# Linear attention and a gated feed-forward block: from the third batch on, k's work runs a pair ahead of q's, z is summed by block turns and spread by DMA, and kv is turned along with q'

## The chip, the cores and the metric

The kernel runs on one core of a Trainium2 chip. The core has five engines that run side by side: TensorE (PE, matrix products, with its weight loads PEld), VectorE (DVE), ScalarE (ACT), GpSimd (POOL) and SyncE (SP), whose only work here is to issue transfers (DMA). Each engine takes its own instructions strictly in order and waits on semaphores for the others. The metric is the device time of one execution in microseconds, as a median of several runs.

## The reference, cut to what matters

```python
# q, k, v: [8 batches, 8 heads, 576 tokens, 64]; omega: [128, 64]
def phi(x):
    h = x @ omega.T - sum(x * x) / 2          # [576, 128]
    return exp(h - max(h)) / sqrt(128)
q_p, k_p = phi(q * scale), phi(k * scale)
kv  = k_p.T @ v                               # [128, 64] of each head
z   = sum(k_p, over the tokens)               # [128]
out = (q_p @ kv) / (q_p @ z + 1e-06)          # [576, 64]
x   = out with heads side by side             # [4608, 512]
y   = ((x @ w_a) * (x @ w_b)) @ w_out         # w_a, w_b: [512, 1536]
```

Everything is float32. The feed-forward products split each operand into two parts (a high and a low one) and add three products.

## The kernel before, in words

Heads are worked on two at a time: a *pair* u = 4 x batch + hp, 32 pairs in all. A pair's 1152 tokens lie as nine chunks of 128, the ninth (the two tails of 64 tokens) shared by the batch in the tiles htk and htq. The feed-forward block of a batch (MoE) needs the x of its four pairs; the attention of the next batch runs beside it, put between the MoE's matmuls.

The order is not written out by hand. The code makes a graph of operations with costs, priorities and buffer slots; `Graph.schedule` (L132) plays it through with its own estimates and writes each engine's instructions in the order that comes out. A margin on an operation (MARGIN, BACK, SUMS) says how much later than its inputs the planner lets it start. SP issues all loads and stores in one queue, in that order.

The steps of a pair in `pair` (L494), for pairs 4 to 31:

- Loads: X holds k and q of the pair with the 64 dimensions on partitions, k on partitions 0 to 63 and q on 64 to 127; natk, natq hold them by token; v.
- `four` (L442): projection, four chunks of k and of q at a time, as products ppk and ppq that run side by side in the two halves of the array; maxima, sums of squares and exp give the tiles hk and hq.
- z: POOL adds hk's chunks (z, zs, six adds), giving 128 partial sums for each feature. ACT and DVE split these into a high and a low part (zr), PE multiplies both by a matrix of ones (pz, L572 and L573), so that the sum over the tokens stands on all partitions, and ACT copies that to zb.
- kv (L588): ten small products into pkv. ACT copies it to k2, PE transposes that (pk, L598), ACT copies it to kl.
- Division: DVE takes the dot product of each chunk of hq with zb (L609, ten for a pair), inverts (L614, L615), and ACT scales hq by it (L619). The result is called q' here.
- The turn of q': DVE turns blocks of 32 x 32 (L627, tile qd), four DMAs write qd to DRAM (qdr, L637), one DMA loads it back into hq, and together that is a transpose. Pair 7 does it on PE instead.
- num: pm (L647) and a short tail (L649) multiply kl with q'. They are not issued alone but right behind the kv products of the next pair (`pending`), so that PE changes to these matmuls once for both. The result goes to the MoE's x.

The MoE of batches 2 to 8 (`moe_block7`) makes products of six matmuls (L1047) in two banks of PSUM, which DVE adds up into c (L1057), and then the output products o (L785). Batch 8 stands for the tails of all.

Of the kernel before, what the change touches and what calls it, by code (L numbers as in the profile page):

```python
# [7 lines left out]
F32 = mybir.dt.float32  # L8
# [9 lines left out]
P = 128  # L18
# [37 lines left out]
class Graph:  # L56
# [3 lines left out]
    def __init__(self):  # L60
        self.ops, self.rings, self.slots = [], {}, {}
# [50 lines left out]
    def place(self, o):  # L112

        t, got = 0, []
        for b in o.alloc:
# [4 lines left out]
            for s in [*ring["slots"], *b.more]:  # L120
# [113 lines left out]
def tile_attention_moe(ctx: ExitStack, tc: tile.TileContext, kqt, kqtt, kqn, kqnt, vx, omst, idn, wab, wout, out):  # L234
# [20 lines left out]
    LATE = dict(wo=["h0", "h1"], ot=["X0", "X1", "h2", "qd0"], owr=["raw0", "raw1"], og=["nat0", "nat1", "ht0", "ht1"], ogf=["xf0", "xf1"],  # L255
# [35 lines left out]
    junk = fixed([P, M], mybir.dt.bfloat16, "junk")  # L291
# [5 lines left out]
    zero = fixed([P, P], mybir.dt.bfloat16, "zero")  # L297
# [69 lines left out]
    qdram = [dram.tile([4, 32, 4, NCH * 32], F32, name=f"qdr{i}") for i in range(3)]  # L367
    qdram_b = [g.buf(None, None, None, f"qdr{i}") for i in range(3)]
    xtd = dram.tile([NHP, P, B * TL], F32, name="xtd")
# [72 lines left out]
    def four(nm, b, pri, x, xdep, dst, c0, sm, sq, al, deps, mg, more):  # L442
# [51 lines left out]
    def pair(u, gate):  # L494
# [59 lines left out]
        def zadd(eng, n, o, a, c, r, w, al=()):  # L554
            g.op({"POOL": pool2(n)}, lambda e: ENG[e].tensor_tensor(o(), a(), c(), op=ALU.add), r=r, w=w, alloc=list(al), prio=pri)  # L555
# [10 lines left out]
        hi, lo = (lambda: zr.ap[:, 0]), (lambda: zr.ap[:, 1])
        g.op({"ACT": act(2 * M)}, copier(hi, lambda: flat(zs)), r=[(zs, None)], w=[(zr, 0)], alloc=[zr], prio=pri + 9)
        g.op({"DVE": dve(2 * M)}, subber(lo, lambda: flat(zs), hi), r=[(zs, None), (zr, 0)], w=[(zr, 1)], prio=pri + 9)
        pz = g.buf("at", [P, 2 * M], F32, f"pz{nm}", more)

        def broadcast(e):
            nc.tensor.matmul(pz.ap[:], ones.ap[:], hi(), start=True, stop=False)  # L572
            nc.tensor.matmul(pz.ap[:], ones.ap[:], lo(), start=False, stop=True)  # L573
        g.op({"PE": mm(2, 2 * M)}, broadcast,
             r=[(zr, None), (ones, None)], w=[(pz, None)], alloc=[pz, zb], prio=pri + 10, margin=mg and mg + CFG["SUMS"])
# [654 lines left out]
```

## Time and profile before

| | us |
|---|---|
| median of three runs | 1074.24 |
| lowest and highest | 1074.06, 1075.35 |
| the profiled execution: its time | 1071.77 |
| the profiled execution: its span | 1070.0 |
| granted TensorE clock, share of full | 1.00 |
| DMA, mean rate | 286 GB/s |

The profile is of one execution. Its page gives the busy time of each engine, forty slices of the span with the busy share in tenths, the chain of work that ended last, and groups of instructions by line, operation and tile with count, busy time, mean length in nanoseconds, and the idle time before them with what ended it. Names of tiles are shown without their numbers: p stands for both MoE banks, c for all sums. Other views answer for one stretch of time (windows, timeline), for one engine's waits, or for one tile.

### The profile page before, as it was taken

To read this page: it belongs to the slowest core of one execution; us is meant where nothing else is said; L and a number is where in the kernel's file an instruction comes from. 1 tells how busy PE (TensorE), PEld (TensorE's weight loads), DVE (VectorE), ACT (ScalarE), POOL (GpSimd) and SP (SyncE) were. 2 spreads that over 40 slices of the span, in tenths; PEclk is the share of its full clock that TensorE was granted. 3 is DMA by queue.
4 is the path that set the end of the run, shared out by engine and by line. 5 is a ranking of instruction groups with operands and counts; after the bars stand their busy time and mean duration, and the time that the engine had idled before them with its cause. 6 is when DMAs were issued, how large, how long until landed. Compare 5 with 4: busy or idle time off the path is not lost.

```text
span 1070.0 us, 22015 instructions
## 1 busy us (share of the span) xinstructions
PE 1053.8 (98%) x7899; PEld 928.8 (87%) x7899; DVE 867.2 (81%) x2145; ACT 591.1 (55%) x1599; POOL 106.4 (10%) x176
## 2 busy tenths in 40 slices
PE   9999999999999999999999999999999999999997
PEld 7878777868788889888888988888888989999997
DVE  6999986989886788777886879778876777998766
ACT  7997767666764646554645566464645423333111
POOL 0021111111110101010111111010101000000000
PEclk9999999999999999999999999999999999999999
DMA  9877966797898888978888888988796799999991
GB/s 359 306 240 230 335 198 208 243 377 274 283 320 295 276 301 269 339 264 289 295 312 295 273 298 270 332 265 299 257 323 196 261 334 304 319 336 344 352 305 50
DMA packets 118270, 305.61 MB, mean 286 GB/s; under 512 B 16656, under 2 KB 35856, under 8 KB 118160
## 3 DMA queue, kind: packets, MB, share of 16 engines
q1 hardware_dynamic: 117296, 303.55, 82.8%
q8 instruction: 62, 1.02, 0.4%
q10 hardware_dynamic: 864, 0.66, 0.2%
q14 instruction: 48, 0.39, 0.1%
HBM read 249.43 MB, written 54.72 MB: 284 GB/s over the span
## 4 chain that ended last, share of the span: by engine, by line
PE 82%; DVE 7%; ACT 5%; DMA 3%; issue 1%; POOL 1%; SPq 0%; ACTq 0%; DVEq 0%
PE p L1047 34%; PE o L785 19%; PE ppk L452 5%; PE pb L956 5%; PE pa L956 5%; PE o_P L853 4%; PE pkv L588 3%; PE pm L647 2%; DMA td<-ts 1%; DVE c L1057 1%; ACT hq L619 1%; ACT hk L486 1%; DMA out_dram<-osb 1%; PE p L853 1%; PE pn L720 1%
## 5 line engine op out<-in xcount | busy, mean ns | idle before, releaser
L1057 DVE TENSOR_TENSOR c<-p,c 128x512 f32<-128x512 f32 (+1 forms) x336 | 207.7, 618 | 93.0 <-PE p L1047 86.7
L785 PE MATMUL o<-wo,ghl 128*128 128x512 f32 x1008 | 270.6, 397 | 0.3 <-DVE ghl L282 0.3
L785 PEld LDWEIGHTS o<-wo,ghl 128*128 128x128 f32 x1008 | 175.5, 188 | 32.0 <-DVE ghl L282 1.2
L1047 PE MATMUL p<-Sa,t 128*128 128x256 f32 x1008 | 144.6, 281 | 1.6 <-ACT c L274 1.6
L1047 PEld LDWEIGHTS p<-Sa,t 128*128 128x128 f32 x1008 | 133.1, 188 | 7.6 <-ACT c L274 2.4
L555 POOL TENSOR_TENSOR z<-hk 128x256 f32<-128x256 f32 x56 | 45.2, 807 | 690.3 <-ACT hk L486 488.9
L274 ACT COPY c<-p 128x256 f32<-128x256 f32 x84 | 31.1, 371 | 125.9 <-PE p L1047 72.7
L486 ACT ACTIVATE hk<-hk,sm 128x128 f32<-128x128 f32 x192 | 62.3, 392 | 46.7 <-DVE sm L482 38.7
L619 ACT ACTIVATE hq<-hq,dn 128x128 f32<-128x128 f32 x224 | 70.6, 392 | 26.6 <-DVE dn L615 24.9
L956 PE MATMUL pb<-x,wb 128*128 128x512 f32 x288 | 75.2, 401 | 0.0
L956 PE MATMUL pa<-x,wa 128*128 128x512 f32 x288 | 73.7, 398 | 0.9 <-DVE x L282 0.9
L1047 PE MATMUL p<-Sb,t 128*128 128x256 f32 x504 | 74.5, 283 | 0.0
L1047 PE MATMUL p<-Sb,bq 128*128 128x256 f32 x504 | 74.5, 283 | 0.0
L1047 PE MATMUL p<-x,t 128*128 128x256 f32 x504 | 73.7, 282 | 0.7 <-ACT oc L274 0.7
L1047 PEld LDWEIGHTS p<-x,t 128*128 128x128 f32 x504 | 69.1, 188 | 5.9 <-ACT oc L274 1.1
L452 PE MATMUL ppk<-om,X 64*128 64x128 f32 x512 | 73.9, 285 | 0.0
L452 PE MATMUL ppq<-om,X 64*128 64x128 f32 x512 | 73.4, 284 | 0.1
L452 PEld LDWEIGHTS ppk<-om,X 64*128 64x128 f32 x512 | 61.7, 187 | 13.5 <-issue 3.4
L1047 PE MATMUL p<-x,wb 128*128 128x256 f32 x504 | 71.2, 284 | 1.6 <-DVE c L1057 1.5
L609 DVE CUSTOM_DVE_ANT_0 junk<-hq,zb 128x128 bf16<-128x128 f32 x224 | 65.6, 293 | 8.6 <-ACT zb L274 6.5
L1047 PE MATMUL p<-x,wa 128*128 128x256 f32 x504 | 71.2, 286 | 1.0 <-DVE c L1057 0.9
L1047 PEld LDWEIGHTS p<-x,wb 128*128 128x128 f32 x504 | 65.9, 188 | 5.1 <-DVE c L1057 2.0
(185 smaller groups left out, 2027.5 us busy)
## 6 DMA issues: line engine op xcount, KB each, us to landing
t<-td SPq DMA_DIRECT2D x168, 512.0 KB, 5.6
wo<-wod SPq DMA_DIRECT2D x96, 512.0 KB, 5.8
bq<-bd SPq DMA_DIRECT2D x84, 256.0 KB, 5.6
X<-in_kqt_dram SPq DMA_DIRECT2D x31, 512.0 KB, 5.7
qdr<-qd SPq DMA_DIRECT2D x108, 144.0 KB, 4.3
hq<-qdr SPq DMA_DIRECT2D x27, 576.0 KB, 6.5
raw<-in_wab_dram SPq DMA_DIRECT2D x24, 512.0 KB, 6.2
td<-ts SPq DMA_DIRECT2D x24, 512.0 KB, 5.9
```

The source lines that it names most:

```text
L274: nc.scalar.copy(o(), i())
L452: nc.tensor.matmul(pps[w].ap[:, c * M:c * M + M], x()[rows, c * P:c * P + P], om.ap[rows], start=True, stop=True)
L486: g.op({"ACT": 392}, lambda e, c=c, w=w: nc.scalar.activation(dst[w].ap[:, c], src[w](c), AF.Exp, scale=SC, bias=sm.ap[:, 2, w, c:c + 1]), ...
L555: g.op({"POOL": pool2(n)}, lambda e: ENG[e].tensor_tensor(o(), a(), c(), op=ALU.add), r=r, w=w, alloc=list(al), prio=pri)
L588: nc.tensor.matmul(pkv.ap[D * j:D * j + D, 0:M], vb.ap[:, vc, 0:D], c(), start=(n == 0), stop=(n == 4))
L609: g.op({"DVE": 413}, lambda e, c=c, j=j, rr=rr, qc=qc: nc.vector.tensor_tensor_reduce(out=junk.ap[rr], in0=qc(), in1=zb.ap[rr, j], scale=1 ...
L619: g.op({"ACT": 392}, lambda e, c=c, src=src: nc.scalar.activation(hq.ap[:, c], src(), AF.Copy, scale=dn.ap[:, c:c + 1]), r=[sd, (dn, None) ...
L785: nc.tensor.matmul(po.ap[:], ghl.ap[:, gi, t * P:(t + 1) * P], wo.ap[:, wi], start=(n == 0 and i == 0), stop=(n == NF - 1 and i == 2))
L853: nc.tensor.matmul(pb.ap[:, t], A[0](ai)[:, t * P:(t + 1) * P], W[0](wi), start=begin and t == j == 0, stop=stop and t == 1 and j == 2)
L956: nc.tensor.matmul(pb.ap[:], wt.ap[:, wi, c], xs[c].at(xi), start=(c == 0 and i == 0), stop=(c == NC4 - 1 and i == 2))
L1047: nc.tensor.matmul(pb.ap[:, half], wcol(wi, c), xc(xi, c), start=n == 0, stop=n == 5)
L1057: g.op({"DVE": dve(n)}, lambda e: nc.vector.tensor_tensor(c4.ap[:, o], pb.ap[:, half], y(), op=ALU.add), r=[*((pb, k) for k in range(half. ...
```

## The change

From pair 8 on (KS = 8, batches 2 to 7) four things differ.

1. *k a pair ahead.* `shifted(u)` projects q of pair u together with k of pair u + 1, and then makes z and kv of pair u + 1. `first_k` makes k of pair 8 alone, one head in each half of the array, and the last pair projects q alone in the same way. The host lays kqt out to match. The tiles h become hk (two, eight chunks) and hq (two, ten chunks). The call that ran the first pair of batch b + 1 ahead of batch b's MoE is gone.
2. *z.* POOL's six adds stay. DVE turns zs by blocks of 32 x 32 into z2 and sums each run of 32, so that each group of 32 partitions has its part of z in zq; ACT copies three groups beside the first, DVE adds the four, one DMA writes 32 x 8 numbers to DRAM (zdr), and one loads the 256 numbers to all partitions (zb). zr, pz and the copy of pz are gone. zb now holds z in another order, and the dot products read it with a step of eight numbers.
3. *kv.* k2 is turned by DVE into a tenth column of qd, goes to DRAM beside q' in four more DMAs with rows of 128 bytes, and comes back in the same load (640 KB instead of 576). pk and kl are gone; num takes kv out of hq's tenth chunk.
4. *Planner.* New margins ZS (800, before z's turn, and before zr in batch 1) and ZB (1500, before the first dot product). Some tiles share slots; `hold` keeps slots from late users until the last q' is turned.

The core of the diff:

```diff
+KS = 2 * NHP
-    for name, n in dict(X=2, Xw=0, nat=2, x2=0, v=2, h=CFG["H"], qd=1, kvz=1, ...
+    for name, n in dict(X=2, Xw=0, nat=2, x2=0, v=2, hk=2, hq=2, qd=1, kvz=0, ...
...
-    qdram = [dram.tile([4, 32, 4, NCH * 32], F32, name=f"qdr{i}") for i in range(3)]
+    qdram = [dram.tile([4, 32, (NCH + 1) * M], F32, name=f"qdr{i}") for i in range(3)]
+    zdram = [dram.tile([32, 8], F32, name=f"zdr{i}") for i in range(3)]
...
+    def first_k(gate):
+        u, mg = KS, CFG["MARGIN"]
...
+        xb = load("X", [P, 4 * P], f"Xk{nm}", lambda: kqt[B - 1, NHP - 1][:, 0:4 * P], early)
...
+        lead = [four(f"k{nm}", b, pr, lambda: xb.ap[:], [(xb, None)], [(hk, 0), (hk, 4)], 0, sm, sq, [hk, sm], gate, mg, [])]
+        last_chunks(b, pr + 5, xe, sqe, [*gate, *lead], mg)
+        zbs[u] = z_sums(u, pr, hk, mg)
+        k2s[u] = kv_burst(u, pr + 40, hk, vb, mg)
...
+    def shifted(u, gate):
...
+        if more:
...
+            for i in range(2):
+                lead = [four(nm, b, pr + 10 * i, lambda i=i: xb.ap[:, 4 * i * P:4 * (i + 1) * P], [(xb, None)], [(hk, 0), (hq, 0)], 4 * i, sm, sq,
+                             [hk, hq, sm] if i == 0 else [], lead, mg, [])]
+            if hp1 == 0:
+                last_chunks(b1, pr + 15, xe, sqe, lead, mg)
+            zbs[u + 1] = z_sums(u + 1, pr, hk, mg)
+        else:
...
+            four(nm, b, pr, lambda: xb.ap[:], [(xb, None)], [(hq, 0), (hq, 4)], 0, sm, sq, [hq, sm], gate, mg, [])
+        divide(u, pr, hq, zbs[u])
+        qT = turn(u, pr, hq, k2s[u])
+        num(u, pr, (lambda j: hq.ap[:, NCH, D * j:D * j + D]), [], qT, mg, more)
+        if more:
+            k2s[u + 1] = kv_burst(u + 1, pr + 40, hk, vb, mg)
...
+        def groups(e):
+            nc.vector.transpose(flat(z2), flat(zs))
+            nc.vector.tensor_reduce(zq.ap[:, 0], flat(z2).rearrange("p (c r) -> p c r", r=32), axis=X, op=ALU.add)
+        g.op({"DVE": 2 * dve(2 * M)}, groups, r=[(zs, None)], w=[(z2, None), (zq, 0)], alloc=[zq], prio=pri, margin=CFG["ZS"])
+        def shift(e):
+            for i in range(1, 4):
+                nc.scalar.copy(zq.ap[0:32, i], zq.ap[32 * i:32 * i + 32, 0])
+        g.op({"ACT": 570}, shift, r=[(zq, 0)], w=[(zq, 1)], prio=pri)
+        g.op({"DVE": 160}, lambda e: nc.vector.tensor_reduce(zq.ap[0:32, 4], zq.ap[0:32, 0:4].rearrange("p i c -> p c i"), axis=X, op=ALU.add),
+             r=[(zq, 0), (zq, 1)], w=[(zq, 4)], prio=pri)
+        g.op({"SP": 330}, dma(lambda: zd, lambda: zq.ap[0:32, 4]), r=[(zq, 4)], w=[(zd_b, None)], prio=-30, nbytes=32 * 8 * 4)
+        zload.append(g.op({"SP": 330}, dma(lambda: flat(zb), lambda: zd.rearrange("r c -> (r c)").partition_broadcast(P)), r=[(zd_b, None)], w=[(zb, None)],
+             alloc=[zb], prio=-30, nbytes=P * 2 * M * 4))
+        return zb, lambda rr, j: zb.ap.rearrange("p j m -> p (j m)").rearrange("p (r j c) -> p j c r", j=2, c=4)[rr, j]
...
+        if k2:
+            g.op({"DVE": dve(M)}, lambda e: nc.vector.transpose(qd.ap[:, :, NCH], k2.ap.rearrange("p (j r) -> p j r", r=32)),
+                 r=[(k2, None)], w=[(qd, 1)], prio=pr + 110)
...
+                if k2:
+                    nc.sync.dma_start(qdr[:, :, NCH * M:].rearrange("j r (i n) -> i r j n", i=4)[i], qd.ap[32 * i:32 * i + 32, :, NCH])
...
-    def attention(b, pairs=range(NHP)):
-        for hp in pairs:
-            pair(NHP * b + hp, [steps[NF * (b - 1) + CFG["GATES"][hp]]] if b > 1 else [])
+    def attention(b):
+        for hp in range(NHP):
+            u = NHP * b + hp
+            gate = [steps[NF * (b - 1) + CFG["GATES"][hp]]] if b > 1 else []
+            if u == KS:
+                first_k(gate)
+            (pair if u < KS else shifted)(u, gate)
```

The order of instructions shows it at three places. First PE, behind the burst that makes kv of pair 20 (batch 5, hp 0) and num of pair 19; p0 and p1 are the MoE's banks, and x, Sa, Sb, t, bq its operands. Before:

```order
L649 MATMUL pkv_5_0_6452<-hq_4_3_5806,kl_4_3_6226 64x64 x2
L1047 MATMUL p1_3610<-x_3_2_4682,wb10_1679 128x256 x3
L1047 MATMUL p1_3610<-x_3_3_4973,wb10_1679 128x256 x3
L1047 MATMUL p1_3610<-Sa_3_0_5033,t3_510_6137 128x256 x3
L1047 MATMUL p1_3610<-Sa_3_1_5045,t3_510_6137 128x256 x3
L572 MATMUL pz_5_0_6499<-zr_5_0_6473,ones_68 128x256
L573 MATMUL pz_5_0_6499<-zr_5_0_6473,ones_68 128x256
L1047 MATMUL p0_3609<-Sa_3_0_5033,t3_510_6137 128x256 x3
L1047 MATMUL p0_3609<-Sa_3_1_5045,t3_510_6137 128x256 x3
L598 MATMUL pk_5_0_6512<-ident_66,k2_5_0_6453 128x128
L1047 MATMUL p0_3609<-Sb_3_0_5095,t3_511_6228 128x256 x3
L1047 MATMUL p0_3609<-Sb_3_1_5112,t3_511_6228 128x256 x3
```

The same burst now, with what follows it:

```order
L787 MATMUL pkv_5_0_6449<-hq_4_3_5883 64x64 x2
L1185 MATMUL p1_3705<-x_3_2_4713,wa10_1614 128x256 x3
L1185 MATMUL p1_3705<-x_3_3_5006,wa10_1614 128x256 x3
L1185 MATMUL p1_3705<-Sa_3_0_5140,t3_500_6154 128x256 x3
L1185 MATMUL p1_3705<-Sa_3_1_5153,t3_500_6154 128x256 x3
L923 MATMUL o3_0_5453<-wo3_9_6197,ghl3_9_6468 128x512 x3
L1185 MATMUL p0_3704<-Sa_3_0_5140,t3_500_6154 128x256 x3
L1185 MATMUL p0_3704<-Sa_3_1_5153,t3_500_6154 128x256 x3
L1185 MATMUL p0_3704<-Sb_3_0_5188,t3_501_6231 128x256 x3
L1185 MATMUL p0_3704<-Sb_3_1_5194,t3_501_6231 128x256 x3
```

pz and pk are gone, and the burst stands one MoE unit earlier (beside wa10 and not wb10). Second SP's queue, where q' of pair 19 goes out and comes back. Before:

```order
L637 DMA qdr1_85<-qd_4_3_6230 32x4x288 x4
L285 DMA t4_000_6283<-td00_100 128x1024
L285 DMA Xe_6_0_6295<-in_kqtt_dram 128x512
L285 DMA bq3_51_6302<-bd51_123 128x512
L285 DMA wo3_11_6324<-wod11_83 128x1024
L285 DMA hq_4_3_5806<-qdr1_85 128x1152
```

Now, from the seventh of the eight writes on:

```order
L769 DMA qdr1_84<-qd19_6174 32x4x288
L772 DMA qdr1_84<-qd19_6174 32x4x32
L286 DMA wo3_8_6310<-wod8_79 128x1024
L286 DMA Xe_5_3_6314<-in_kqtt_dram 128x512
L286 DMA natee_5_3_6335<-in_kqnt_dram 128x512
L286 DMA natk_5_3_6348<-in_kqn_dram 128x512
L286 DMA hq_4_3_5883<-qdr1_84 128x1280
L286 DMA t3_511_6379<-td51_113 128x1024
L286 DMA zdr2_88<-zq_5_0_6355 32x8
```

Eight writes stand where four stood, the load back takes kv with it, and the write of z (with its load some rows later) is new. Third DVE, among the dot products of pair 20 (batch 5, hp 0; a dot product and the reading of its sum are two rows of the name ISA; c3_51 is a MoE sum):

```order
L736 ISA zero_70,dn_5_0_6549<-hq_5_0_6299,zb_5_0_6447 128x128
L736 ISA dn_5_0_6549 128x1
L687 STREAM_TRANSPOSE z2_5_1_6529<-zs_5_1_6530 128x256
L688 TENSOR_REDUCE zq_5_1_6590<-z2_5_1_6529 128x8
L736 ISA zero_70,dn_5_0_6549<-hq_5_0_6299,zb_5_0_6447 128x128
L736 ISA dn_5_0_6549 128x1
L736 ISA zero_70,dn_5_0_6549<-hq_5_0_6299,zb_5_0_6447 128x128
L736 ISA dn_5_0_6549 128x1
L695 TENSOR_REDUCE zq_5_1_6590<-zq_5_1_6590 32x8
L1195 TENSOR_TENSOR c3_51_6593<-p1_3705,c3_51_6593 128x2x256
```

The sums of z of pair 21 now stand among the dot products of pair 20, where before a pair's zr stood ahead of its own dot products.

More of the change, by code (lines that the diff above doesn't have):

```diff
@@ L119, in place @@
             best = None
-            for s in [*ring["slots"], *b.more]:
+            for s in [*ring["slots"], *(x for x in b.more if x not in self.hold or self.hold[x].end is not None)]:
                 if any(s == y for _, y in got):
@@ L535, in pair @@
             at = 4 * i - x0
-            lead = [four(nm, b, pr + 10 * i, lambda xb=xb, at=at: xb.ap[:, at * P:(at + 4) * P], [(xb, None)], h, 4 * i, sm, sq,
+            lead = [four(nm, b, pr + 10 * i, lambda xb=xb, at=at: xb.ap[:, at * P:(at + 4) * P], [(xb, None)], [(t, 0) for t in h], 4 * i, sm, sq,
                          [*h, sm] if i == 0 else [], [*gate, *lead], mg, more)]
@@ L540, in pair @@
                 ends[b] = [g.buf("ht", [P, NHP, M], F32, f"ht{'kq'[w]}{nm}") for w in range(2)]
-                lead = [four(f"e{nm}", b, pr + 5, lambda: xe.ap[:], [(xe, None)], ends[b], 0, sme, sqe, [*ends[b], sme], [*gate, *lead], mg, more)]
-        he = ends[b]
+                lead = [four(f"e{nm}", b, pr + 5, lambda: xe.ap[:], [(xe, None)], [(t, 0) for t in ends[b]], 0, sme, sqe, [*ends[b], sme],
+                             [*gate, *lead], mg, more)]
         if hp == 0:
@@ new lines, in pair @@
+        g.op({"ACT": act(2 * D)}, copier(lambda: kl.ap[:], lambda: pk.ap[:]), r=[(pk, None)], w=[(kl, None)], prio=pr + 40)
+        divide(u, pr, h[1], zb)
+        if u in CFG["TURN"]:
+            t = pe_transposes(nm, pr, mg, more, [(lambda c=c: h[1].ap[:, c], (h[1], c)) for c in range(NCH)])
+            qT = t, lambda j: t.ap[:, 5 * j:5 * j + 4], lambda j: t.ap[:, 4, TL * j:TL * j + TL]
+        else:
+            qT = turn(u, pr, h[1])
+        num(u, pr, (lambda j: kl.ap[:, j]), [(kl, None)], qT, mg)
@@ new lines, in load, with natural @@
+    def load(ring, shape, name, src, prio):
+        t = g.buf(ring, shape, F32, name)
+        n = 4
+        for k in shape:
+            n *= k
+        g.op({"SP": 330}, dma(lambda: t.ap[:], src), w=[(t, None)], alloc=[t], prio=prio, nbytes=n)
+        return t
+    def natural(srcs, nm, pr, b):
+        tiles = [load("nat", [P, *shape], f"nat{k}{nm}", lambda src=src: src, pr - 1400 + i + 1) for i, (k, src, shape) in enumerate(srcs)]
+        sq = g.buf("sq", [P, 2, 8 // (3 - len(srcs))], F32, f"sq{nm}")
+        if len(srcs) == 1:
+            square_sums([(tiles[0], lambda: sq.ap.rearrange("p w c -> p (w c)"), None)], sq, 8, nm, pr, b, True)
+        else:
+            square_sums([(tiles[w], lambda w=w: sq.ap[:, w], w) for w in range(2)], sq, 8, nm, pr, b, True)
+        return sq
@@ L566, in pair @@
[L566 to L573, printed above, removed]
@@ L582, in pair @@
-        pkv = g.buf("at", [P, M + TL], F32, f"pkv{nm}", more)
         def kvmm(e):
@@ L1157, in tile_attention_moe @@
         if b + 1 < B:
-            attention(b + 1, range(int(ahead), NHP))
+            attention(b + 1)
     flush(100 * len(steps))
```

210 lines of the change are left out of this document (138 added, 72 removed).

## The prediction

> **What bounds the kernel now.** I read the page's busy times and slices first, then the windows by stage, then what TensorE (PE) waited for, and last its timeline.
>
> ```profile
> PE 1053.8 (98%) x7899; PEld 928.8 (87%) x7899; DVE 867.2 (81%) x2145; ACT 591.1 (55%) x1599; POOL 106.4 (10%) x176
> PE   9999999999999999999999999999999999999997
> DVE  6999986989886788777886879778876777998766
> ```
>
> PE is busy in every slice but the last; VectorE (DVE) has idle time in most slices. PE idles 16.2 us in all (1070.0 less 1053.8), so nearly all of the time is PE's work. In the windows by stage (length, then busy time of PE, PEld, DVE, ACT, POOL, then the granted clock, the DMA share and GB/s) there is one weak stretch:
>
> ```profile
> 200.00:240.00 40.00, 39.00 (x226) 29.99 (x224) 36.20 (x87) 24.08 (x63) 4.53 (x6) 1.00 0.95 337
> 240.00:280.00 40.00, 39.42 (x233) 31.01 (x233) 37.94 (x106) 26.93 (x70) 4.27 (x6) 1.00 0.81 284
> 280.00:320.00 40.00, 38.24 (x274) 32.48 (x271) 34.41 (x87) 30.92 (x84) 6.82 (x12) 1.00 0.91 300
> 520.00:560.00 40.00, 39.35 (x301) 35.45 (x301) 31.87 (x88) 22.10 (x59) 5.22 (x9) 1.00 0.86 298
> ```
>
> From 200 to 320 us DVE is busy 108.6 of 120 us and PE loses 3.3; in the middle DVE has a fifth to spare. The clock is 1.00 throughout. PE's own waits (total, times, longest):
>
> ```profile
> PE p L1047 <- DVE c L1057: 2.4, 4, 1.5
> ...
> PE pz L572 <- ACT k L274: 1.6, 1, 1.6
> ...
> PE pm L647 <- ACT hq L619: 0.7, 1, 0.7
> ```
>
> They are few and short. So a change pays here by what it takes off PE's list of work, and costs by any new wait it puts into that list.
>
> **The change part by part: PE.** From pair 8 on (24 of the 28 pairs that use this path) the two broadcast matmuls pz and the transpose pk go. The timeline of PE round one pair (start, length, line, tiles) prices them:
>
> ```profile
> 523.67 0.87 PE L1047 MATMUL p<-Sa,t 128*128 128x256 f32 x6
> 524.38 0.29 PE L572 MATMUL pz<-zr,ones 128*128 128x256 f32 x1
> 524.50 0.28 PE L573 MATMUL pz<-zr,ones 128*128 128x256 f32 x1
> 524.62 0.87 PE L1047 MATMUL p<-Sa,t 128*128 128x256 f32 x6
> 525.33 0.27 PE L598 MATMUL pk<-ident,k 128*128 128x128 f32 x1
> 525.36 0.96 PE L1047 MATMUL p<-Sb,t 128*128 128x256 f32 x6
> 526.15 0.87 PE L1047 MATMUL p<-x,t 128*128 128x256 f32 x6
> ```
>
> Lengths overlap, so the spacing of starts counts. A product of six takes 0.71 us (523.67 to 524.38). pz holds PE from 524.38 to 524.62: 0.24 us. From pk's start to the product after next is 0.82 us (525.33 to 526.15), 0.11 more than one product: pk costs 0.11 to 0.12 us. I take 0.36 us a pair, and 24 x 0.36 = **8.6 us** off PE. All other PE work is kept: the projection of k alone for pair 8 uses both halves of the array with one head each, as does that of q alone for pair 31, so the number of projection bursts is the same; num still rides on the kv burst of the next pair.
>
> Of the waits above, the 1.6 us of pz falls at 240 to 280 us, in batch 2, and its place disappears. What is late next there is the product behind it; I count half, 0.8 us (bounds 0 and 1.6).
>
> **DVE.** Rows of before that price what is added and removed (busy, mean ns):
>
> ```profile
> L627 DVE STREAM_TRANSPOSE qd<-hq 128x1152 f32<-128x1152 f32 x27 | 37.0, 1370 | 2.2 <-ACT hq L619 2.2
> L439 DVE TENSOR_REDUCE sq<-natq 128x8 f32<-128x512 f32 x31 | 21.0, 676 | 3.6 <-ACT natq L437 3.5
> L282 DVE TENSOR_TENSOR zr<-zs,zr 128x256 fp32r<-128x256 f32 x28 | 11.7, 416 | 8.4 <-ACT zr L274 8.4
> L609 DVE CUSTOM_DVE_ANT_0 junk<-hq,zb 128x128 bf16<-128x128 f32 x224 | 65.6, 293 | 8.6 <-ACT zb L274 6.5
> L329 DVE SCALAR_TENSOR_TENSOR raw<-raw 128x512 int32<-128x512 int32 x36 | 24.8, 698 | 0.1
> ```
>
> Between 512 columns (676) and 256 (416) lie 260 ns, about 1.02 ns a column. Then the turn of z (256 columns) is an estimate of 1370 - 896 x 1.02 = 0.46 us, that of kv (128) 0.33, the sum of 256 columns 0.41, the small sum under 0.2; removed is 0.42. Net about +1.0 us a pair, 24 us in all, DVE 867 to 891. In the middle this lies in idle time. In 200 to 320 us, where batch 2's four pairs and the first of batch 3 run, 5 x 1.0 = 5 us meet 11.4 us of idle DVE; I take 1.5 us of new PE loss there, about half of what that stretch loses today (bounds 0 and 5).
>
> The dot products (L609) now read z with a step of eight numbers, 32 bytes. No row of before reads so. L329 steps by 8 bytes and costs 698 for 512, as contiguous rows do, so the low bound is 293 unchanged; doubling the 128 elements adds 128 x 1.02 = 0.13 us each, ten a pair, 1.3 us, as the high bound, a rival below. I take none, by L329. The Trainium skill, "SBUF — State Buffer", section "Door 1: The DMA port swizzle", speaks against it: SBUF lines are 16 bytes, two hits a line are needed for full rate, and four fp32 is as far as one strides for free. L329 has two hits a line and agrees; no row tests a step of 32 bytes. By that rule the high bound would hold and the sum be some 3 us higher.
>
> **ScalarE (ACT).** Three passes go, three small copies come:
>
> ```profile
> L274 ACT CAST zr<-zs 128x256 fp32r<-128x256 f32 x28 | 11.4, 406 | 15.2 <-POOL zs L555 15.0
> L274 ACT COPY zb<-pz 128x256 f32<-128x256 f32 x28 | 10.5, 374 | 33.4 <-PE pz L573 33.3
> L274 ACT COPY kl<-pk 128x128 f32<-128x128 f32 x28 | 7.5, 269 | 13.7 <-PE pk L598 13.7
> L274 ACT COPY xts<-pkv 128x64 f32<-128x64 f32 x26 | 5.8, 221 | 0.0
> ```
>
> 406 + 374 + 269 - 3 x 221 = 0.39 us less a pair, 9 us in all; at 55% busy it is worth nothing on the path.
>
> **Queue and transfers.** SP issues six more DMAs a pair: four for kv, one out and one in for z.
>
> ```profile
> L637 SPq DMA_DIRECT2D qdr<-qd x108: 303/439/1646, 97.9 to 855.4; - x108
> L285 SPq DMA_DIRECT2D hq<-qdr x27: 319/320/728, 101.8 to 859.0; - x27
> qdr<-qd SPq DMA_DIRECT2D x108, 144.0 KB, 4.3
> hq<-qdr SPq DMA_DIRECT2D x27, 576.0 KB, 6.5
> xtd<-xts SPq DMA_DIRECT2D x8, 128.0 KB, 4.6
> ```
>
> At 439 ns each the eight writes take 3.5 us instead of 1.8, so the load back of q' is issued some 1.8 us later; t, wo and bq loads queue behind. The kv rows are 128 bytes; the nearest row is xtd, rows of 256 bytes, which lands in 4.6 us against 4.3 for long rows, so small rows alone cost little. Bytes grow by about 64 + 64 + 128 KB a pair, 6 of 306 MB. What must cover this is the slack before num. One of the worst pairs of before, num's start and the landing of its load:
>
> ```profile
> 499.85 1.08 PE L647 MATMUL pm<-hq,kl 128*64 128x512 f32 x4 [0.74 <-ACT hq L619]
> L285 SPq DMA_DIRECT2D hq<-qdr x1: 319/319/319, 492.1 to 492.1; - x1
> DMA to landing us min/median/max: 7.6/7.6/7.6
> ```
>
> It landed at 499.7 and PE waited 0.74 us (the engine named had long been done; it was the DMA). The planner places the burst by its own time for these transfers, which it now takes longer, and k, z and kv are made a pair (27 back loads from 101.8 to 859.0 us: 757/26 = 29 us) ahead, so I let these waits stand as they are: 0, with bounds of -0.7 (gone) and 23 x 0.74 = 17 (every joint burst as bad as this one).
>
> **Sum.** -8.6 - 0.8 + 1.5 = -7.9 us. Against the profiled execution (span 1070.0, time 1071.77) that is 1063.9; that execution lies 2.5 us below the median of the runs shown, 1074.24, on which I put the forecast: **1066.3 us**.
>
> **The rivals.**
> - *Strided reads cost double.* For it: z's step of 32 bytes is four times that of the only strided row. The Trainium skill's rule above says the same. DVE then has 1.3 us a pair more to do, 32 us. In the middle it is covered: the sum c of one product ended while PE came back to that bank much later.
>
> ```profile
> 491.75 0.69 DVE L1057 TENSOR_TENSOR c<-p,c 128x512 f32<-128x512 f32 x1
> 492.36 0.28 DVE L609 CUSTOM_DVE_ANT_0 junk<-hq,zb 128x128 bf16<-128x128 f32 x1
> ...
> 493.35 0.29 DVE L609 CUSTOM_DVE_ANT_0 junk<-hq,zb 128x128 bf16<-128x128 f32 x1
> ...
> 493.72 0.69 DVE L1057 TENSOR_TENSOR c<-p,c 128x512 f32<-128x512 f32 x1
> ...
> 494.21 0.87 PE L1047 MATMUL p<-x,t 128*128 128x256 f32 x6
> ```
>
> The add is done at 492.44 and its bank is written again at 494.21: 1.8 us of slack, against 4 x 0.13 = 0.5 us from the four dot products that stand between this add and the next (492.36 to 493.35). In the crowded stretch 5 x (1.0 + 1.3) = 11.5 us meet 11.4 us idle, so I add 3 us there: about 1069. Chance 0.14.
> - *Z comes late.* The first dot product waits on DVE for two DMAs in a row, and the adds c queue behind it. Two landings like xtd's are 9.2 us. Against it stands the pair of lead, 29 us. If DVE is held so long that a third of a microsecond a pair passes the 1.8 us of slack, 24 x 0.33 = 8 us eats the gain: about 1074. Chance 0.11.
> - *The load back of q' becomes the bound.* Eight writes, small rows, then one load of 640 KB. If the burst has not moved by as much, each of 23 joint bursts waits. The point from which it decides is 8.6/23 = 0.37 us a burst; at 0.74, as in the row above, 17 - 8.6 = +8.4: about 1082, slower. Against it: the pair quoted was among the worst, and PE's waits list pm once. Chance 0.13.
> - *As summed*: 1062 to 1070, chance 0.62.
>
> **How the numbers follow.** About 0.2%, 2.1 us, is what a measurement of this kernel can tell from no change. Faster takes the forecast and the strided rival, 0.76; same the late z, 0.11; slower the load back, 0.13. The low end is 8.6 + 1.6 + 0.7 = 10.9 us off with a little more, 1062; the high end takes in both rivals that end at or below 1074, and a little of the third: 1075.
>
> **What would show it.** Right: PE's busy time falls by 8 to 9 us, its idle time stays at 14 to 18 us, no pz or pk in batches 2 to 7. The dot product's mean says which bound holds: 293 or about 420 ns. The late z shows as DVE waiting on zb from DMA; the load back as PE waiting at pm on hq, many times. The forecast fails if PE's idle time grows by more than a few us, whoever is named, or if PE's work does not fall.

## The result, and the profile after

The changed kernel takes 1085.29 us in the median of 6 runs (1083.02 to 1089.74), the kernel before 1073.69 us in 6 runs beside them. The ratio is 1.0112, 95% interval 1.0091 to 1.0134: slower by 12 us, where 7.9 us faster was forecast. (A thousandth of a ratio is 1.07 us below.) The profiled execution of after took 1087.76 us, span 1086.0; before 1071.77, span 1070.0. The ratios here and below leave out four executions that were far slower than the rest of their kernel (one of e17, three of the kernel before beside e13 to e16, all over 1140 us).

The busy times of after:

```profile
PE 1056.0 (97%) x7827; PEld 925.0 (85%) x7827; DVE 903.5 (83%) x2193; ACT 594.2 (55%) x1623; POOL 104.5 (10%) x176
```

PE has 72 matmuls fewer, as planned, and yet is busy 2.2 us longer; its idle time went from 16.2 to 30.0 us (1086.0 less 1056.0). So its work did shrink, and more than the gain came back, as waits and as matmuls that took longer. DVE rose by 36 us instead of 24. The waits of PE that grew (total, times, longest):

```profile
PE p L1185 <- DVE c L1195: 6.4, 9, 1.4
PE pm L785 <- DMA hq<-qdr: 3.8, 5, 1.9
PE ppq L454 <- DVE x L283: 2.5, 3, 1.3
PE o L923 <- DVE ghl L283: 1.8, 2, 1.0
PE o L923 <- ACT osb L275: 1.7, 1, 1.7
```

No single wait stands out: PE is late for DVE (c, ghl, x), for the load back of q' (hq) and for ScalarE. The dot product in the costliest groups, and the transfers of a pair (KB each, median us to landing):

```profile
L736 DVE CUSTOM_DVE_ANT_1 zero<-hq,zb 128x128 bf16<-128x128 f32 x192 | 78.4, 408 | 14.0 <-DMA zb<-zdr 8.3
```

```profile
hq<-qdr SPq DMA_DIRECT2D x24, 640.0 KB, 7.6
...
zb<-zdr SPq DMA_DIRECT2D x24, 128.0 KB, 4.3
...
zdr<-zq SPq DMA_DIRECT2D x24, 1.0 KB, 4.9
```

The dot products cost 408 ns instead of 293, and DVE waits 8.3 us for z to come by DMA; the back load lands 7.6 us after its issue instead of 6.5. There is one more loss, which no list of waits shows. PE's timeline at the last pair's num (what it waited for in brackets), and the windows of 1 us behind it (length, busy PE, PEld, DVE, ACT, POOL, then the granted clock, DMA share, GB/s):

```profile
864.01 1.28 PE L785 MATMUL pm<-hq 128*64 128x512 f32 x4 [1.90 <-DMA hq<-qdr]
```

```profile
863.00:864.00 1.00, 0.00 (x0) 0.02 (x1) 0.00 (x0) 0.00 (x0) 0.00 (x0) 1.00 1.00 412
864.00:865.00 1.00, 0.99 (x4) 0.38 (x6) 0.00 (x0) 0.00 (x0) 0.00 (x0) 0.88 1.05 414
865.00:866.00 1.00, 1.00 (x8) 0.87 (x5) 0.06 (x1) 0.68 (x2) 0.00 (x0) 0.50 0.98 401
866.00:867.00 1.00, 1.00 (x7) 1.00 (x6) 0.79 (x2) 0.02 (x1) 0.00 (x0) 0.50 0.28 107
867.00:868.00 1.00, 1.00 (x4) 0.81 (x3) 0.89 (x2) 0.00 (x0) 0.00 (x0) 0.50 0.60 148
868.00:869.00 1.00, 1.00 (x9) 0.90 (x9) 1.00 (x3) 0.00 (x0) 0.00 (x0) 0.92 0.03 7
```

PE idles 1.9 us, and within 1 us of having work again its clock falls to 0.50 for some 3.4 us. That costs another 1.7 us (0.12 + 3 x 0.50 + 0.08) and is booked as busy time. It happens twice in this execution, here and at 233 us behind a wait of 1.3 us: 3.4 us in all; in the profiled execution of before the clock falls only in the last microsecond of the span. The dips are not the bulk of the loss: one of the six runs of after has a mean clock of 1.000, and it took 1084.59 us.

### The profile page after: what moved, and what is told of

It is laid out like the page before. It is cut to its first block, busy times and chain, and to the rows that moved or that the text cites. A ratio compares the mean times of both kernels' runs of the same rounds, so it can differ in the third digit from the quotient of the medians.

```text
span 1086.0 us, 22246 instructions
## 1 busy us (share of the span) xinstructions
PE 1056.0 (97%) x7827; PEld 925.0 (85%) x7827; DVE 903.5 (83%) x2193; ACT 594.2 (55%) x1623; POOL 104.5 (10%) x176
## 4 chain that ended last, share of the span: by engine, by line
PE 41%; DVE 13%; DMA 11%; issue 2%; ACT 2%; SPq 0%; DVEq 0%; ACTq 0%
PE p L1185 24%; PE o L923 8%; DVE c L1195 4%; PE o_P L991 3%; DMA hq<-qdr 3%; DMA zb<-zdr 2%; DVE zero L736 2%; PE ppk L454 2%; DMA out_dram<-osb 2%; DMA t<-td 2%; PE pm L785 1%; PE pkv L715 1%; DMA zdr<-zq 1%; DVE c L1234 1%; DVE ghl L283 1%
## 5 line engine op out<-in xcount | busy, mean ns | idle before, releaser
L923 PE MATMUL o<-wo,ghl 128*128 128x512 f32 x1008 | 273.6, 399 | 3.7 <-DVE ghl L283 1.8
L736 DVE CUSTOM_DVE_ANT_1 zero<-hq,zb 128x128 bf16<-128x128 f32 x192 | 78.4, 408 | 14.0 <-DMA zb<-zdr 8.3
L490 ACT ACTIVATE hk<-hk,sm 128x128 f32<-128x128 f32 x184 | 59.7, 392 | 30.0 <-DVE sm L485 29.6
L275 ACT CAST ghl<-c 128x512 fp32r<-128x512 f32 (+1 forms) x72 | 41.0, 587 | 60.2 <-DVE c L1234 51.3
```

The source lines that it names most:

```text
L275: nc.scalar.copy(o(), i())
L490: g.op({"ACT": 392}, lambda e, c=c, w=w, to=to, at=at: nc.scalar.activation(to.ap[:, at + c], src[w](c), AF.Exp, scale=SC, bias=sm.ap[:, 2 ...
L736: g.op({"DVE": 413}, lambda e, c=c, j=j, rr=rr, qc=qc: nc.vector.tensor_tensor_reduce(out=cols(junk.ap[rr]), in0=cols(qc()), in1=zcol(rr, ...
L923: nc.tensor.matmul(po.ap[:], ghl.ap[:, gi, t * P:(t + 1) * P], wo.ap[:, wi], start=(n == 0 and i == 0), stop=(n == NF - 1 and i == 2))
```

## The experiments

Three theories stood at the start. A: the dot products' step makes DVE late. B: the transfers (z by DMA, the longer trip of q') do it. C: it is the new order itself, k a pair ahead.

### The step of 32 bytes: e1 and e2

e1 keeps everything and takes the step away, at the price of one small turn a pair on DVE; e2 puts the step into the kernel before. Neither moves another instruction.

```diff
# e1
+            nc.vector.transpose(zt.ap[:], zq.ap[0:32, 1:5].rearrange("p i c -> p (i c)"))
-        g.op({"SP": 330}, dma(lambda: zd, lambda: zq.ap[0:32, 4]), ...
+        g.op({"SP": 330}, dma(lambda: zd, lambda: zt.ap[24:32]), ...
-        return zb, lambda rr, j: ...rearrange("p (r j c) -> p j c r", j=2, c=4)[rr, j]
+        return zb, lambda rr, j: zb.ap.rearrange("p j (c r) -> p j c r", r=32)[rr, j]
# e2, in the kernel before
-  copier(lambda: zb.ap.rearrange("p j m -> p (j m)"), lambda: pz.ap[:])
+  copier(lambda: ...rearrange("p (r j c) -> p j c r", j=2, c=4), lambda: pz.ap.rearrange("p (j c r) -> p j c r", j=2, c=4))
```

> The changed kernel, but z comes back in natural order, so that the dot products read it without a step: the 32x8 sums are turned once more on DVE (one 32x32 block turn a pair) and go out as 8 rows of 128 bytes; the order of all engines is that of the changed kernel but for this one turn. Theory A (the dot products with a step of 32 bytes, 408 ns instead of 293, make DVE late, and PE waits for c, ghl and x): dot mean back to 285 to 295 ns, DVE busy time 903.5 to about 880, PE idle 30 to about 20 us, time 1066 to 1073. Theory B (transfers: z by DMA and the later load back of q'): dot mean falls too, but the time stays at 1081 to 1086. Theory C (the new order of PE's work itself): the same, 1081 to 1086.

> The kernel before with z written in the permuted order by its ScalarE copy and read with a step of 32 bytes by the dot products of the 28 pairs; the order of all engines is that of the kernel before. Theory A: DVE busy time 867 to about 897 (10 x 28 x 0.115 = 32 us), and PE idle grows by 8 to 20 us, time 1081 to 1093. Theories B and C: the crowd of DVE is not what PE waits for, time 1073 to 1077.

Measured: e1 1.0049 (1.0031 to 1.0068), 1079.54 us; e2 1.0061 (1.0044 to 1.0078), 1081.44 us. The busy times and the dot products among the costliest groups, e1 first:

```profile
PE 1052.5 (98%) x7827; PEld 924.4 (86%) x7827; DVE 883.8 (82%) x2217; ACT 594.1 (55%) x1623; POOL 104.5 (10%) x176
...
L740 DVE CUSTOM_DVE_ANT_0 zero<-hq,zb 128x128 bf16<-128x128 f32 x224 | 66.0, 295 | 13.2 <-DMA zb<-zdr 4.7
```

```profile
PE 1057.9 (98%) x7899; PEld 930.8 (86%) x7899; DVE 897.9 (83%) x2145; ACT 596.5 (55%) x1599; POOL 104.6 (10%) x176
...
L610 DVE CUSTOM_DVE_ANT_1 junk<-hq,zb 128x128 bf16<-128x128 f32 x224 | 93.3, 416 | 12.0 <-ACT zb L274 9.6
```

From both sides the step is worth 6 to 7 us (0.0063 and 0.0061): theory A holds, but for half of the loss. e1 missed its range, since 5 us of loss and 25.2 us of idle PE stay. Some 20 us (after less e1) or 31 us (e2 less before) more on an engine that is 81 to 83% busy cost 6.5 us: the rest of DVE's time is not free. e2 met its time, but not the mechanism expected: PE's idle time grew by 3.8 us (to 20.0) and not by 8 to 20, and PE's wait for c stayed (2.3 us, 2.4 before), so it isn't c that carries the delay, as theory A had it. What grew is ScalarE's wait for the divisors dn, in before and in e2:

```profile
ACT hq L619 <- DVE dn L615: 24.9, 9, 4.7
```

```profile
ACT hq L620 <- DVE dn L616: 35.5, 17, 5.4
```

Behind it q' goes out later, and PE waited 2.3 us at pm for its load back (0.7 before). The step is also recorded as another form (ANT_1), a two-level pattern; whether the step or the pattern costs was not separated.

### Chance, and k ahead alone: e3 and e4

e3 changes one margin (ZB=1500 to 1600). e4 undoes the other two parts: z through pz for all pairs (`if u < KS:` becomes `if True:`, zr in the slot of qd), and kv through PE:

```diff
# e4
-        qT = turn(u, pr, hq, k2s[u])
+        pk = g.buf("at", [P, M], F32, f"pk{nm}")
+        g.op({"PE": 108}, lambda e: nc.tensor.transpose(pk.ap[:], k2s[u].ap[:], ident.ap[:]), ...
+        g.op({"ACT": act(M)}, copier(lambda: hq.ap[:, NCH], lambda: pk.ap[:]), ...
+        qT = turn(u, pr, hq)
```

> The changed kernel with the planner's margin for z (ZB) 1600 in place of 1500, which puts some 180 of 2566 rows of PE in other places and alters no work. Theories A and B: 1083 to 1088, as the changed kernel. Theory C in its weak form (the time hangs on chance in the order the planner finds): off the changed kernel's 1085.3 by over 4 us, either way.

> Only k a pair ahead of q: z is summed and spread by two matmuls pz and read without a step, kv is turned by TensorE (pk) and put beside q' by a ScalarE copy, both as in the kernel before; no small DMAs. Theory C (k ahead of q itself costs): 1080 or more, since pz and pk are back on PE (8.6 us) and the loss stays. Theories A and B: the loss goes with the stride and the transfers; the time is that of the kernel before, 1070 to 1077, with waits of PE for hq and DVE as few as before.

Measured: e3 1.0115 (1.0090 to 1.0140), the changed kernel again: moving these rows doesn't undo the loss. e4 1.0092 (1.0071 to 1.0114), 1084.73 us: k ahead alone costs 9.9 us, with pz and pk on PE, no step and no small transfers. Theory C holds for a large part.

e4 is not quite k ahead and nothing else. Every engine gets a new order, it keeps the slots and margins of the changed kernel, and zr, which has a buffer of its own in before, lies in the slot of qd. There ScalarE waits for the writes of qd, which it never does in before:

```profile
ACT zr L275 <- DMA qdr<-qd: 9.2, 4, 5.3
```

The waits of PE within 3 us behind these four add up to 0.3 us, so little of the loss follows from them directly; what the shared slot does to the order was not tested. Nor are the waits of PE the whole loss:

```profile
PE 1059.4 (98%) x7899; PEld 930.0 (86%) x7899; DVE 865.8 (80%) x2128; ACT 595.5 (55%) x1616; POOL 105.6 (10%) x176
```

The same 7899 matmuls keep PE busy 5.6 us longer than in before (1053.8), and its idle time grew by 8.4 us (to 24.6). Why the matmuls took longer stays open.

Its waits of PE, beside those of before (pz 1.6, pk 0.3), sit at the two PSUM banks "at" that projections, kv, num and pk share:

```profile
PE pk L640 <- DVE x L283: 3.2, 3, 1.7
PE p L1189 <- DVE c L1199: 2.7, 8, 0.5
PE ppk L454 <- ACT hk L275: 2.6, 2, 1.5
PE pk L640 <- ACT xts L275: 1.3, 1, 1.3
...
PE pkv L719 <- ACT hk L275: 1.1, 1, 1.1
```

Two mechanisms behind them can be read in e4's trace. First, ScalarE (its timeline, and below it its wait for the store of an output tile, in before and in e4):

```profile
797.17 0.59 ACT L275 COPY hq<-ppq 128x512 f32<-128x512 f32 x1
802.19 0.59 ACT L275 COPY osb<-o 128x512 f32<-128x512 f32 x1 [4.42 <-DMA out_dram<-osb]
802.67 1.28 ACT L490 ACTIVATE hk<-hk,sm 128x128 f32<-128x128 f32 x4
803.85 1.27 ACT L490 ACTIVATE hq<-hq,sm 128x128 f32<-128x128 f32 x4
805.02 0.57 ACT L275 COPY hk<-ppk 128x512 f32<-128x512 f32 x1
```

```profile
ACT osb L274 <- DMA out_dram<-osb: 8.1, 6, 1.8
```

```profile
ACT osb L275 <- DMA out_dram<-osb: 19.4, 8, 4.4
```

The copy of an output tile waits 4.4 us at the head of ScalarE until an earlier store has left its buffer. The exps and the copy that frees the projection's bank stand behind it (the bank is freed at 805.6), and PE waits there 1.1 us for kv and, 6 us later, 1.7 at pk for an x that comes behind the next exps. Second, POOL beside DVE:

```profile
361.18 1.57 DVE L283 TENSOR_TENSOR ghl<-c,ghl 128x512 fp32r<-128x512 f32 x1
```

```profile
361.05 0.45 POOL L660 TENSOR_TENSOR zs<-zs,htk 64x128 f32<-64x128 f32 x1
361.46 0.73 POOL L660 TENSOR_TENSOR z<-hk 128x256 f32<-128x256 f32 x1
```

The subtraction takes 1.57 us instead of 0.7 as its like. Every DVE instruction of before and of e4 that ran over 0.1 us longer than the median of its like ran beside a POOL add: 47 of them with some 14 us, 55 with some 19 us.

### Stores and POOL's adds: e5 to e8, and a mend: e9 and e11

e5 to e8 take each mechanism away in e4 and, as control, in before, with the order unchanged: e5 and e6 leave most of each output row unwritten, e7 and e8 leave z out. e9 and e11 leave nothing out, but the planner writes a new order.

```diff
# e5, e6
-  dma(lambda: out[b * S + t * P:b * S + (t + 1) * P, :], lambda: osb.ap[:])
+  dma(lambda: out[b * S + t * P:b * S + (t + 1) * P, 0:16], lambda: osb.ap[:, 0:16])
# e7, e8
-  nc.gpsimd.tensor_tensor(o(), a(), c(), op=ALU.add)
+  nc.gpsimd.memset(o() if len(r) == 1 else o()[..., 0:1], 1.0)
# e9, e11: Graph.slot_free
-        return t
+        return t + (3000 if b.ring == "osb" else 0)
```

> k ahead alone (e4), but the 28 stores of o (osb) write 16 of 512 columns only, which leaves out most of those output rows; the order of all engines is that of e4. Theory O (a copy osb at the head of ScalarE waits for the store that still reads its buffer, and the copies that free the projection's PSUM banks, the exps and the bursts of PE stand behind it): ACT's waits for out_dram fall from 19.4 us to under 8, and the time falls from 1084.7 by 4 to 8 us, to 1077 to 1081. Theory P (POOL's sums of z hold up DVE at worse places) and theory C (the two banks alone): ACT's waits fall too, but the time by less than 2 us, 1083 to 1086.

> The control of e5: the kernel before with the same small stores, its order unchanged. Theory O: its waits for out_dram are 8.1 us with 1.8 at the longest, so little is to be had: 1072 to 1075. If it falls as much as e5 does (to 1070 or less), small stores help everywhere by moving less, and e5 says nothing of k ahead.

> k ahead alone (e4), but POOL's six adds of z a pair are replaced by short fills with 1.0 (z is left out: constant); the order of all engines is that of e4. Theory P (every DVE instruction that took over 0.1 us more than its like ran beside a POOL add, 17.5 us in e4 and 13.9 us before; with k ahead these fall on instructions that PE waits for): DVE's busy time falls by 15 to 18 us and the time by 4 to 8 us, to 1077 to 1081. Theories O and C: the time falls by 0 to 3 us, 1082 to 1085.

> The control of e7: the kernel before with the same fills in place of POOL's adds, its order unchanged. Theory P: DVE's busy time falls by 13 to 14 us, the time by 0 to 3 us, 1071 to 1075. If it falls as much as e7 does, the adds cost the same in both orders and don't explain what k ahead costs.

> k ahead alone (e4) with one line of the planner changed: it takes a buffer osb as free 3000 (its ns) later than before, near what the stores' landings show (4.5 to 5.7 us in the median), so it puts the next copy osb later on its engine; no work is left out. Theory O, from e5 (1.0092 to 1.0046 with small stores): ACT's waits for out_dram fall from 19.4 us to under 6, ratio to before 1.003 to 1.006, 1077 to 1081. If the wait only moves (the copy osb frees the o bank late, and PE waits at o), the ratio stays at 1.008 or more.

> Control of e9: the kernel before with the same line of the planner. Its waits for out_dram are 8.1 us; by e6 (small stores: 0.9989) there is about 1 us to be had: 0.997 to 1.001.

| | k ahead alone | 95% | before | 95% | difference |
|---|---|---|---|---|---|
| as it is (e4) | 1.0092 | 1.0071 to 1.0114 | 1 | | 9.9 us |
| small stores (e5, e6) | 1.0046 | 1.0034 to 1.0057 | 0.9989 | 0.9978 to 0.9999 | 6.1 us |
| no POOL adds (e7, e8) | 1.0031 | 1.0020 to 1.0043 | 0.9961 | 0.9949 to 0.9974 | 7.5 us |
| store slack (e9, e11) | 1.0047 | 1.0035 to 1.0059 | 0.9964 | 0.9951 to 0.9977 | 8.9 us |

The differences carry some 2 us of uncertainty, and what a row takes off the first row some 3. Both mechanisms are real: with either gone, k ahead alone gains 5 to 6.5 us. But the kernel before gains too, and only the difference counts for the change: 3.8 us by e5 and e6, 2.4 us by e7 and e8, the latter not clear of noise. e8's fall of 4.2 us lies above its expectation. It has a second cause beside DVE's delays, for the fills are shorter than the adds (POOL busy 19.8 us, 106.4 before), and 15.0 us that ScalarE waits in before at zr for POOL are gone too; in e4 that wait is 1.5 us. Of the expectations on waits, e5's was missed (ACT's wait for stores fell to 10.7 us, not under 8), e9's was met:

```profile
ACT osb L275 <- DMA out_dram<-osb: 1.2, 2, 0.6
```

e9 got the ratio that theory O named, but its control e11 gained 3.9 us where about 1 was expected, so by this pair theory O explains 1 us of the 9.9, and by e5 and e6 3.8. If the two add up, between 4 and 7 us of what k ahead costs stay unexplained; they are spread over many short waits at the two banks and for c. That the bursts ask for these banks at worse places is argued, not shown: a third bank was not tried.

### z, kv, and the line in which they stand: e12, e10, e13 to e18

e12 is e1 with e4's edit for kv, and came out between its two ranges. e10 is e1 with e9's line, e13 is e9 with kv through DRAM (e4 without its edit for kv), e14 is e12 with e9's line. e15 and e16 are e10 and e14 with ZB=4000. e17 and e18 are e10 and e15 with kv on an early trip of its own:

```diff
# e17, e18
+    def kv_trip(u, pr, hq, k2):
+        ... nc.vector.transpose(blocks(hq.ap[:, NCH]), blocks(k2.ap[:])) ...
+            for i in range(4):
+                nc.sync.dma_start(kdr.rearrange("j r (i n) -> i r j n", i=4)[i], blocks(hq.ap[32 * i:32 * i + 32, NCH]))
+        g.op({"SP": 400}, dma(lambda: hq.ap[:, NCH], lambda: kdr.rearrange("j r n -> (j r) n")), ...
-        qT = turn(u, pr, hq, k2s[u])
+        kv_trip(u, pr, hq, k2s[u])
+        qT = turn(u, pr, hq)
```

> The changed kernel with z in natural order (e1), but kv turned by TensorE (pk) and put beside q' by a ScalarE copy as in e4: no kv writes through DRAM, q' alone goes as 4 writes of 288 columns and comes back as 576 KB. Against e1 (1.0049). pk costs PE 24 x 0.115 = 2.8 us. Theory B (the eight writes and the later load back cost): PE's waits at pm and the waits behind SP's queue fall by more than that, ratio 1.000 to 1.004. If the DRAM trip of kv costs nothing: 2.8 us more, ratio 1.006 to 1.009.

> The changed kernel with z in natural order (e1) and the same line of the planner as e9: the two mended costs together. If they add up: e1's ratio of 1.0049 less the 0.004 to 0.005 that e5 showed, 0.999 to 1.002, 1072 to 1076; ACT's waits for out_dram fall from 20.2 us to under 6. If the order's chances outweigh it: 1.004 or more.

> k ahead with the store slack of e9, z by PE as in e9 (pz, natural order), but kv through DRAM as in the changed kernel: only the kv trip differs from e9 (1.0047) in the work, and only the z trip from e10 (1.0118). Theory Z (z by DMA is what spoils e10: DVE stands at zb, the adds c behind it): ratio 1.002 to 1.007, near e9. Theory K (the eight writes and the later load back spoil it): near e10, 1.009 to 1.013, with PE waiting at pm for hq.

> The other half: store slack, z by DMA in natural order, kv turned by TensorE (e12 with store slack). Theory Z: near e10, 1.007 to 1.012, DVE waits for zb over 8 us. Theory K: near e9 less pz's 5.8 us of PE, 0.998 to 1.003.

> e10 with the planner's margin behind z's load (ZB) 4000 in place of 1500, near the two landings measured (4.9 and 4.3 us): the first dot product is put later. Theory Z: DVE's wait for zb falls from 14.0 to under 4 us and the ratio from 1.0118 to 1.000 to 1.006. Theory K: the ratio stays over 1.008.

> e14 with the same margin of 4000 behind z's load. Theory Z: DVE's wait for zb under 4 us, ratio 0.998 to 1.004; the best of the versions with k ahead. Theory K: no better than e14.

> e10 (natural z by DMA, store slack) with kv still through DRAM, but on a trip of its own: turned on DVE as soon as kv and hq's place for it are there, four writes and a load of 64 KB, early in the pair; q' alone goes as in the kernel before (4 writes, 576 KB back). Theory K1 (the loss comes from standing in line with q'): the load back of q' lands 2 us or more ahead of num, PE's waits at pm fall from 3.3 to under 1.5 us, no dip of the clock, ratio from 1.0118 to 0.995 to 1.001. Theory K2 (small packets and crowding as such): 1.007 or more.

> e17 with the planner's margin of 4000 behind z's load (e15: 1.0043, and e16 with kv on PE: 0.998). Theory K1: by e16 less pk's 2.8 us of PE, 0.994 to 0.999, at or below the best version so far with k ahead. Theory K2: 1.003 or more.

All with z in natural order and k ahead:

| z by | kv by | store slack | ratio | 95% |
|---|---|---|---|---|
| PE | PE | no (e4) | 1.0092 | 1.0071 to 1.0114 |
| DMA | PE | no (e12) | 1.0041 | 1.0029 to 1.0053 |
| DMA | DRAM with q' | no (e1) | 1.0049 | 1.0031 to 1.0068 |
| PE | PE | yes (e9) | 1.0047 | 1.0035 to 1.0059 |
| DMA | PE | yes (e14) | 0.9988 | 0.9977 to 1.0000 |
| PE | DRAM with q' | yes (e13) | 1.0110 | 1.0090 to 1.0130 |
| DMA | DRAM with q' | yes (e10) | 1.0118 | 1.0091 to 1.0144 |
| DMA | DRAM, own trip | yes (e17) | 0.9979 | 0.9968 to 0.9990 |

e16 (e14 with the later dot product) gives 0.9980 (0.9969 to 0.9991), e18 0.9983 (0.9966 to 1.0000), e15 1.0043 (1.0025 to 1.0060). e10 came out 10 us above the sum that it tested, where its expectation had put the chances of the order (1.004 or more). e13 and e14 say more, against theory Z that had been put first. Where z goes by DMA instead of PE with kv on PE, the kernel gains 5.5 us (e4 to e12) or 6.3 (e9 to e14), near pz's 24 x 0.24 = 5.8 (zr and its waits go with it); with kv in line with q' it gains nothing (e13 to e10). Wherever kv goes in line with q', the kernel loses: 0.9 us (e12 to e1, within the noise), 6.8 (e16 to e15), 14 (e14 to e10), though pk's 2.8 us are saved each time. The 6.8 us of e9 to e13 say less, since zr shares the slot of qd there, and ScalarE's waits at zr for transfers grew from 10.3 to 21.1 us.

The sign is the same each time, but the size hangs on the order, which is new in each of these kernels. The same line of store slack gained 3.9 us in before, 4.8 in e4 and 5.7 in e12, and lost 7.4 in e1 (e10). Part of the loss is dips of the clock: the runs of e13 have mean clocks of 0.993 to 0.997, those of e9 and e14 0.998 to 1.000, and 0.003 of 1085 us is some 3 us. The waits of PE at num, e13 and then e14:

```profile
PE pm L785 <- DMA hq<-qdr: 5.9, 5, 1.8
```

```profile
PE pm L793 <- DMA hq<-qdr: 0.6, 2, 0.4
```

The distance from the end of DVE's turn of q' over a pair to the landing of its back load and to num's start is, in the mean of the last 24 pairs: before 13.0 and 15.9 us, after 17.6 and 18.8, e13 15.3 and 16.6. The slack ahead of num fell from 2.9 to 1.2 us. (Of the back loads of e12 and e17 the trace has 4 and 8 landings only; their issue is known, 6.8 and 7.5 us behind the turn, against 6.7 in before and 10.0 in after.) In after's last pair the trip looks so (SP's queue; the turn ends at 849.7):

```profile
849.73 0.44 SPq L769 DMA_DIRECT2D qdr<-qd  x1
...
853.79 0.30 SPq L772 DMA_DIRECT2D qdr<-qd  x1
856.09 0.32 SPq L286 DMA_DIRECT2D hq<-qdr  x1
```

Eight writes take 4.4 us, the back load goes out at 856.1 and lands 7.8 us later, 1.9 after PE came for it. e17 keeps every byte of kv's trip and takes it out of this line: num starts 16.0 us behind the turn, and in the 8 pairs whose landing is known the load lands 2.0 us ahead of it, as theory K1 expected. Its busy times, and PE's wait at num:

```profile
PE 1050.0 (98%) x7827; PEld 923.0 (86%) x7827; DVE 889.0 (83%) x2221; ACT 591.8 (55%) x1619; POOL 105.9 (10%) x176
```

```profile
PE pm L805 <- DMA hq<-qdr: 0.8, 1, 0.8
```

The ratio falls from 1.0118 to 0.9979, and with the later dot product from 1.0043 (e15) to 0.9983 (e18). So it is the place in line and not the packets, as far as two pairs of kernels with new orders can show it. Of pk's 2.8 us little is to be seen: e17 is 1.0 us below e14, within the noise. What stays loose is e15: the later dot product gained 8 us on e10, as theory Z said, with DVE's wait for zb gone (14.0 us before) but PE still waiting 5.1 us at pm; in e14 to e16 the same margin gave nothing that can be measured.

The best version is neither of the two kernels as given: e11, the kernel before with one line of the planner, 0.9964, 1069.39 us. Of those with k ahead e17 is the best, 2 us faster than before; it has the same line of the planner and is 1.6 us behind e11, so nothing is left that the change itself gains.

## Why the prediction was wrong, point by point

- **The moved order was not priced at all: the step that failed first.** The text said "All other PE work is kept" and gave k's place a pair ahead no term but cover. The matmuls are kept in number, but k ahead costs 9.9 us (e4, with the slots of the changed kernel): PE's waits grew, and the same matmuls kept it busy 5.6 us longer. Stores at ScalarE's head make 1 to 4 us of it, POOL's adds some 2, each give or take 3; the rest is open.
- **The dot products at 293 ns, "by L329".** They took 408. The row chosen stepped by 8 bytes and could not speak for 32; the Trainium skill's rule, which the prediction set aside ("SBUF — State Buffer", section "Door 1: The DMA port swizzle", four fp32 for free), agrees with the 408 ns, as far as step and pattern can't be told apart. The high bound of 0.13 us each was right (0.115).
- **The rival for it had the mechanism right and the size too small.** It added 3 us to the forecast; e1 and e2 show 6 to 7. Its cover, 1.8 us between c and the reuse of its bank, was real for c (e2: 2.3 us of waits, 2.4 before), but DVE's lateness goes on through dn to ScalarE and q', which had no cover in the sum.
- **PE: right in size.** pz's 5.8 us came back as 5.5 and 6.3; pk's 2.8 were not seen by themselves. In the changed kernel itself nothing of it is to be seen, since waits and two stretches at half clock fill PE's time; busy time was the wrong sign to look for.
- **"I let these waits stand as they are: 0".** The argument was that the planner knows the longer trip and that k, z and kv are a pair ahead; but kv was put into q's trip, not ahead of it. Without store slack the net is 0.9 us, or 3.7 with pk's 2.8 put back; in other orders 9.6 (e16 to e15) and 17 (e14 to e10), the end of the bounds, 17. The load back goes out 3.3 us later (10.0 us behind the turn, 6.7 before) where 1.8 was priced. The rival with 1082 us named this mechanism; it had the chance 0.13. That its number lies near the 1085 measured is luck: PE waited at pm 5 times and 3.8 us, not 23 times and 17.
- **The small terms of the sum, -0.8 for pz's wait and 1.5 for the crowded stretch,** are not what failed. From 200 to 320 us PE idles 3.3 us before, 3.6 in after and 3.0 in e1. The rows that DVE gained cost what they were priced at (435, 298, 420 and 188 ns). ScalarE was 3 us busier than before and not 9 less, for which the runs name no cause; at 55% busy nothing hangs on it.
- **Late z** was a real wait (8.3 us of DVE in after), but what it costs is not settled: nothing in e14 to e16, up to 8 us in e10 to e15.

The sum by runs, each step against the one before it: k ahead +9.9 (e4), z by DMA -5.5 (e12), kv in line with q' +0.9 (e1), the step of 32 bytes +6.8 (after): +12.1 us. That these add up to the 12 measured is so by construction, as each step starts from the one before it; only the last keeps the order.

## What to carry to other kernels

Where PE is busy 98% of the time, an edit that moves work needs a price for its new neighbours: on every engine in order, ask which instruction will stand at its head waiting for a transfer, and what behind it frees a bank. A transfer that can start early should not be joined to one that is on the way to the next matmul, however few bytes it adds. And undoing all parts but one, with the order of the others as control, found in one run (e4) what no list of waits in the changed kernel showed. Where a planner writes a new order for every edit, one pair of kernels doesn't price an edit: look for the same sign in several pairs, and see what else shares a buffer.

## What the runs showed of the hardware

- A wait of PE can cost more than itself. In after, e1, e3, e10 and e13 gaps of 1.3 to 2.4 us were followed, 0.6 to 1.7 us after PE had work again, by about 3.4 us at a clock of 0.50 (1.7 us lost, twice that in e13, where two gaps lay close). Other gaps were not: 1.58 us in before, 1.70 in e4, 1.70 at 445 us in after. The Trainium skill, "TensorE: Matmul & The Clock Gate", section "Part 1: The HAM clock gate (the "warmup" mystery)", has half rate and windows of 3.4 us that run freely, which agrees with the length of the dips and would make it chance which gaps are hit; it asks for an idle window of about 3.4 us, while here 1.3 us were enough.
- POOL's adds held up single DVE instructions by up to 0.97 us. The Trainium skill, "SBUF — State Buffer", section "Who interferes with whom", has the two share a port pair as an exclusive lock; e7 and e8 agree, with no DVE instruction over 0.1 us late once the adds are gone. The kernel is then 4.2 us faster before and 6.5 with k ahead, which prices the adds as a whole and not the sharing alone.
- A write of 1 KB in 32 rows took 4.9 us to land in the median, longer than the writes of 144 KB (3.5), with the DMA engines busy over 80% of the time.
